# An attention-and-experts kernel: half block emptied by ACT, G two chunks later, the slot's search later, and the second layer two chunks behind the first

## The chip, the core and the metric

The kernel runs on one core of a Trainium2 chip. Of that core's engines the text uses these names: PE is the matrix engine (matmuls; its weight loads are shown apart as PEld), DVE the vector engine, ACT the scalar engine, POOL the general engine, SP the engine that issues most loads. Each engine works through its own list of instructions in the order in which they stand there. The metric is the device time of one execution in microseconds (us); lower is better.

## The reference

Two stages follow each other. The first is a Nystrom attention over 8 batches, 8 heads, 576 tokens and 64 numbers a head:

```python
A = sm(q, k_lm); Bm = sm(q_lm, k_lm); C = sm(q_lm, k)      # 32 landmarks
Z = Bm.transpose(0, 1, 3, 2) / (norm_1 * norm_inf + 1e-06)
for _ in range(6):
    Z = 2 * Z - Z @ Bm @ Z
attn_out = A @ Z @ C @ v
```

The second sends each token (512 numbers, all heads side by side) through one of 8 experts. A token takes the expert with the largest logit when it is the first of its batch or when its local gate is below 0.5, and otherwise keeps the expert of the token before it:

```python
h = np.maximum(x[b, s] @ w1[e], 0.0)        # 512 -> 1024
out[b, s] = p[e] * (h @ w2[e])              # 1024 -> 512
```

## The kernel before

**Batches and chunks.** The expert stage takes one batch after the other (`for b in range(B)`, B = 8). A batch is computed with one expert, the one that most of its tokens chose (`own`). Tokens that chose another are gathered over all batches into a "slot" of 128 rows that runs after batch 7 as a ninth, smaller expert (`sts[B]`). Further slots would follow in a loop at the end.

A batch's 576 tokens are done in two passes (`PASSES`): first 320 tokens, which are the output blocks 2 and 3 of 128 tokens and block 4 of only 64, the **half block**; then 256 tokens, blocks 0 and 1. Each pass has 8 **chunks** f, one for every 128 of the 1024 hidden numbers, so a batch has 16 chunks (`CH`). The text numbers them 0 to 15 within a batch, and b*16 + i over all. The slot has 8 chunks of 128 tokens.

**One chunk.** `mm1` (L525 on) is the first layer: six matmuls (L534) of weights `gh`, `gl` and tokens `ath`, `atl` into a bank of `ph`, of which there are two. High and low parts of a number are separate, so three products stand for one. ACT (L541) takes the positive part into `h`, DVE (L544, L547) its low part. `after` (L561 on) is the second layer: with the weights `wh`, `wl` of that chunk it adds three products for each full block to that block's `py` bank (L570), and for the half block two products to the one `pg` bank (L579), where 64 rows hold the high and 64 the low part. In `expert`, `before` holds the second layer of the preceding chunk: the program states the first layer of chunk f, then the second layer of chunk f-1. At the end of a batch `before()` finishes the last one.

**G.** Attention's last product is never formed by itself: `w_w1` (L487) multiplies the expert's `w1` by a small matrix of the batch into G, in two halves of 512 hidden numbers. Each half takes 16 matmuls (L498) into one `pg` bank and one `ph` bank, and two casts on ACT and two subtractions on DVE (L511, L512) empty them. As the `pg` bank is also the half block's, the first of these matmuls carries a dependency on the last reader of `pg`, kept in `reader["pg"]`. `G_AT` names the chunks of a batch at which the next batch's halves are stated.

**The store.** After the last chunk of a pass, `store` scales each block by the token's gate and writes it out. Full blocks are scaled by ACT (L593). For the half block DVE copies the 64 low rows out of `pg` (L596) and adds the 64 high ones (L597), then ACT scales (L599) and its queue issues the transfer. `ys` has two buffers.

**Weights.** `load_w2` loads a chunk's second-layer weights on SP's queue; ACT casts them to `wh` (L521) and POOL subtracts to get `wl` (L522). `get_w2` is called some chunks ahead.

**Attention beside it.** Attention of batch b+1 is cut into some 35 steps, put at chunk times in `events` by `at_time` and run just before the chunk whose time has passed (`run`). So are the slot's steps: `others` (L603) ranks the leftover tokens of all batches in a long row of DVE instructions, and `slot_tokens` (L669) searches the tokens of one slot in five pieces: the slot's batch and expert (`xregs`); a mask, then five `row` tiles of DVE (L695) with 8 matmuls each (L698) into one bank; addresses from it and 8 gathers on POOL (L721); two transposes on PE (L727); casts. `slot_weights` (L734) reads `xregs` on SP and loads that expert's `w1`.

**The order.** `schedule_with_timeline_sim=True`: what the program states is a priority, not the order. When the kernel is built, the order of every engine's list is settled with modelled durations: what the model holds ready goes first, the earlier stated first among these. `not_ahead_of` ties an instruction behind a marked one of its engine.

Of the kernel before, what the change touches and what calls it, by code (L numbers as in the profile page):

```python
# [9 lines left out]
F32 = mybir.dt.float32  # L10
F32R = mybir.dt.float32r
# [46 lines left out]
def nystrom_attn_then_sticky_moe(ctx, tc, qT, kT, v, wg, w12, out):  # L58
# [414 lines left out]
        nc.vector.tensor_mul(st["pw"], s[:, 0], s[:, 1])  # L473


    reader = {}

    def expert_of(reg):
        return nc.values_load(reg, engines=[ET.SP], min_val=0, max_val=E - 1,
# [45 lines left out]
    def mm1(st, f, s0, n, apart):  # L525

        hp = ph.tile([P, 512], F32, name="ph")[:, 0:n]
        gh, gl = st["g", f // 4]
        ah, al = st["at"]
        c = slice(f % 4 * P, f % 4 * P + P)  # L530
        i = 0
        for g in range(2):
            for w, x in ((gh, ah), (gh, al), (gl, ah)):
                nc.tensor.matmul(hp, w[:, g, c], x[:, g, s0:s0 + n], start=(i == 0), stop=(i == 5))  # L534
                i += 1

        m = n // P * P
        h = fk.tile([P, 640], F32R, name="h", bufs=3)
        x = fk.tile([P, P], F32R, name="hx", bufs=NC2) if apart and m < n else h[:, 2 * P:3 * P]
        e = m if apart else n  # L540
        nc.scalar.activation(out=h[:, 0:e], in_=hp[:, 0:e], func=AF.Relu)  # L541
        if e < n:
            nc.scalar.activation(out=x[:, 0:64], in_=hp[:, m:n], func=AF.Relu)
        nc.vector.scalar_tensor_tensor(out=h[:, 384:384 + m], in0=hp[:, 0:m], scalar=0.0, in1=h[:, 0:m].bitcast(F32),  # L544
                                       op0=ALU.max, op1=ALU.subtract)
        if m < n:
            nc.vector.scalar_tensor_tensor(out=x[:, 64:128], in0=hp[:, m:n], scalar=0.0, in1=x[:, 0:64].bitcast(F32),  # L547
                                           op0=ALU.max, op1=ALU.subtract)
        return h, x

    def expert(st, w2, passes, store, apart=False):

        before = None
        for s0, n, blocks in passes:
            yps, hs = {}, {}
            for f in range(NC2):
                hs[f] = mm1(st, f, s0, n, apart)
                if before:
                    before()

                def after(f=f, blocks=blocks, yps=yps, hs=hs):  # L561
                    full = [k for k in blocks if k < 4]
                    for k in full:
                        if k not in yps:
                            yps[k] = py.tile([P, DM], F32, name="py")
                    wh, wl = w2[f]
                    h = hs[f][0]
                    for part, w in ((0, wh), (0, wl), (384, wh)):
                        for i, k in enumerate(full):
                            nc.tensor.matmul(yps[k], h[:, part + i * P:part + i * P + P], w, start=(f == 0 and part == 0 and w is wh),  # L570
                                             stop=(f == NC2 - 1 and part == 384))
                    if 4 in blocks:


                        for ff in range(0 if f == NC2 - 1 else NC2, NC2) if apart else (f,):
                            if 4 not in yps:
                                yps[4] = pg.tile([P, DM], F32, name="pg")
                            for w in w2[ff]:
                                nc.tensor.matmul(yps[4], hs[ff][1], w, start=(ff == 0 and w is w2[ff][0]),  # L579
                                                 stop=(ff == NC2 - 1 and w is w2[ff][1]))  # L580
                    if f == NC2 - 1:
                        for k in blocks:
                            store(k, yps[k])

                before = after
                yield
        before()

    def store(b, st, k, yp):
        ys = fk.tile([P, DM], F32, name="ys", bufs=2)  # L590
        t0 = b * S + k * P
        if k < 4:
            nc.scalar.mul(out=ys, in_=yp, mul=st["pw"][:, k:k + 1])  # L593
            nc.scalar.dma_start(out=out[t0:t0 + P, :], in_=ys)
        else:
            nc.vector.tensor_copy(out=ys[0:64], in_=yp[64:128])  # L596
            last = nc.vector.tensor_tensor(out=ys[0:64], in0=ys[0:64], in1=yp[0:64], op=ALU.add)  # L597
            reader["pg"] = last.ins.name
            nc.scalar.mul(out=ys[0:64], in_=ys[0:64], mul=st["pw"][0:64, k:k + 1])  # L599
            nc.scalar.dma_start(out=out[t0:t0 + 64, :], in_=ys[0:64])  # L600


# [63 lines left out]
        xs.update(slot=slot, lo=lo, base=base, end=end, now=now, tabp=tabp)  # L666
        yield

    def slot_tokens(st):  # L669

        now = xs["now"]
        nc.vector.tensor_scalar_add(now, now, 1.0)
# [20 lines left out]
        for c0 in range(0, NCOL, 8):  # L693
            row = xp.tile([P, 8, P], BF16, name="row")
            nc.vector.tensor_tensor(out=row, in0=iota128.unsqueeze(1).broadcast_to([P, 8, P]),  # L695
                                    in1=xs["lo"][:, c0:c0 + 8].unsqueeze(2).broadcast_to([P, 8, P]), op=ALU.is_equal)
            for c in range(8):
                nc.tensor.matmul(pi, row[:, c, :], rhs[:, c0 + c, :], start=(c0 + c == 0), stop=(c0 + c == NCOL - 1))  # L698
        yield
        pf = xp.tile([P, 7], F32, name="pf")  # L700
        nc.vector.tensor_copy(out=pf, in_=pi)
# [22 lines left out]
        yield  # L724
        px = one.tile([P, 2, P])
        for g in range(2):
            nc.tensor.transpose(out=px[:, g, :], in_=xa[:, g].rearrange("p c l -> p (c l)"), identity=ident)  # L727
        st["at"] = [xp.tile([P, 2, P], F32R, name=f"xa{p}") for p in "hl"]
        nc.scalar.copy(out=st["at"][0], in_=px)
        nc.vector.tensor_tensor(out=st["at"][1], in0=px, in1=st["at"][0].bitcast(F32), op=ALU.subtract)  # L730
# [19 lines left out]
    def whole_slot():  # L750
# [9 lines left out]
        for f in range(NC2):  # L760
            w2[f] = load_w2(st["e"], f)
            next(gen)
        for _ in gen:
            pass


    sts = [{} for _ in range(B + 1)]
# [29 lines left out]

    CH, SPAN, END = 2 * NC2, 24, 4

    G_AT = (NC2 + 3, NC2 + 6)  # L800
    events = []

    def at_time(t, fn):
# [11 lines left out]
    def slots_begin():  # L815
        nonlocal xp
        lctx.close()
        xp = ctx.enter_context(tc.tile_pool(name="xp", bufs=1, side="right"))
        gens.extend([others(), slot_tokens(sts[B])])

    def slots_end():
        for _ in gens[1]:
            pass
        sts[B]["e"] = slot_weights(sts[B])

    xp, gens = None, []
    at_time((B - 2) * CH + END + 1, slots_begin)
    for i in range(4):
        at_time((B - 2) * CH + END + 2 + i, lambda: next(gens[0], None))
        at_time((B - 2) * CH + END + 6 + i, lambda: next(gens[1], None))  # L830
    at_time((B - 1) * CH + END + 0.5, slots_end)
    events.sort()

    def run(t):
# [17 lines left out]
    for b in range(B):  # L852
        st = sts[b]
        gen = expert(st, w2s[b], PASSES, lambda k, yp, b=b, st=st: store(b, st, k, yp), b == 0)
        for i in range(CH):
            if i < 2:
                get_w2(b, NC2 - 2 + i)
            elif i >= NC2 + 2:
                get_w2(b + 1, i - NC2 - 2)
            run(b * CH + i)  # L860
            if b == 0 and i == 2:

                w_w1(st, 1)
            if i in G_AT:
                w_w1(sts[b + 1], G_AT.index(i))
            next(gen)
        for _ in gen:
            pass
    run(B * CH)


    st = sts[B]
    gen = expert(st, w2s[B], ((0, P, (0,)),), lambda k, yp: slot_store(st, k, yp))
    for f in range(NC2):
        if f < 2:
            get_w2(B, NC2 - 2 + f)
        next(gen)
    for _ in gen:
        pass
    n_slots = nc.values_load(nslot[0:1, 0:1], min_val=0, max_val=E * B * 5)  # L880
    with tc.If(n_slots > 1):
        with tc.For_i(1, n_slots):
# [31 lines left out]
```

## Time and profile before

| what | us |
|---|---|
| median of three runs | 537.75 |
| lowest and highest | 537.05 and 537.84 |
| the profiled execution | 535.65 |
| its span, first to last instruction | 533.9 |
| PE busy in the span | 486.3 |
| DVE, ACT, POOL busy | 309.3, 209.6, 188.9 |

The profile is of one execution, taken by the chip's own recorder. Rows of a timeline give the start (us from the span's start), the duration, engine, line and operation, what it writes and reads, and in brackets the engine's idle time just before with what ended it. Rows of the waits give a sum in us, how often, and the longest. Rows of grouped lines give count, busy us, mean ns of one, idle us before. Windows give the busy us of each engine in a stretch, then the granted PE clock (1.00 is full speed) and transfers. Matmuls overlap, and their ends are modelled: the distance between starts is what one costs PE.

### The profile page before, as it was taken

The page shows a single profiled execution, that of the slowest core. Times are in us where ns is not written, and L with a number is a line of the kernel's source. Part 1 is how long each engine was busy: PE and PEld are TensorE (multiplying, and loading weights), DVE is VectorE, ACT ScalarE, POOL GpSimd, SP SyncE. Part 2 cuts the span into 40 slices and gives each one's busy share as a digit, 9 for nine tenths or more (in the row PEclk, how much of TensorE's full clock was granted, in tenths as well). Part 3 has the DMA queues.
Part 4 walks back from the last instruction along what each step waited for, and adds up shares of the span by engine and source line. Part 5 has one row for each costly group of instructions (what it writes and reads, how often), then busy time and mean ns, then how long its engine had stood idle before and what let it go on. Part 6 is the DMA issues. An engine that isn't in the chain of part 4 may idle for free. (4 is left out here: it accounts for less than half of the span.)

```text
span 533.9 us, 12288 instructions
## 1 busy us (share of the span) xinstructions
PE 486.3 (91%) x4791; PEld 349.9 (66%) x4791; DVE 309.3 (58%) x955; ACT 209.6 (39%) x529; POOL 188.9 (35%) x203
## 2 busy tenths in 40 slices
PE   6657569999999999999999999999998998799994
PEld 1325236866687577767786668657775787487784
DVE  7887837843587366834695368436653358752321
ACT  2333262444334451535245433354154412441451
POOL 5565270543126320643046301322133300563240
PEclk9775569999999999999999999999999999799999
DMA  8844760971159412961089010931083106371310
GB/s 300 328 147 172 247 211 6 372 262 40 51 183 355 139 51 69 376 231 51 3 325 329 24 50 28 353 119 51 1 284 109 68 1 223 128 267 44 109 60 19
DMA packets 38605, 82.59 MB, mean 155 GB/s; under 512 B 3163, under 2 KB 4443, under 8 KB 37776
## 3 DMA queue, kind: packets, MB, share of 16 engines
q1 hardware_dynamic: 30656, 66.22, 35.7%
q10 hardware_dynamic: 6400, 10.49, 5.4%
q0 software_dynamic: 1488, 5.07, 2.4%
q8 instruction: 39, 0.64, 0.5%
q14 instruction: 22, 0.18, 0.1%
HBM read 66.34 MB, written 15.47 MB: 153 GB/s over the span
## 5 line engine op out<-in xcount | busy, mean ns | idle before, releaser
L570 PE MATMUL py<-wh,h 128*128 128x512 f32 x528 | 177.4, 409 | 3.6 <-ACT h L541 2.9
L522 POOL TENSOR_TENSOR wl<-raw,wh 128x512 fp32r<-128x512 f32 x72 | 93.3, 1301 | 175.9 <-ACT wh L521 169.5
L541 ACT ACTIVATE h<-ph 128x256 fp32r<-128x256 f32 (+2 forms) x136 | 54.7, 403 | 146.7 <-PE ph L534 144.1
L570 PEld LDWEIGHTS py<-wh,h 128*128 128x128 f32 x528 | 91.4, 188 | 31.6 <-ACT h L541 12.8
L544 DVE SCALAR_TENSOR_TENSOR h<-ph,h 128x256 fp32r<-128x256 f32 (+1 forms) x136 | 55.3, 409 | 69.2 <-ACT h L541 68.0
L570 PE MATMUL py<-wl,h 128*128 128x512 f32 x264 | 88.1, 396 | 0.0
L534 PE MATMUL ph<-ath,gh 128*128 128x320 f32 (+1 forms) x256 | 79.1, 309 | 2.1 <-ACT gh L511 2.1
L534 PE MATMUL ph<-atl,gh 128*128 128x320 f32 (+1 forms) x256 | 76.6, 299 | 0.0
L534 PE MATMUL ph<-ath,gl 128*128 128x320 f32 (+1 forms) x256 | 76.1, 297 | 0.0
L521 ACT CAST wh<-raw 128x512 fp32r<-128x512 f32 x72 | 44.7, 620 | 54.4 <-PE py L570 40.3
L534 PEld LDWEIGHTS ph<-ath,gh 128*128 128x128 f32 x256 | 48.8, 191 | 19.7 <-issue 6.7
L570 PEld LDWEIGHTS py<-wl,h 128*128 128x128 f32 x264 | 49.5, 188 | 10.7 <-issue 1.3
L362 POOL TENSOR_TENSOR sa<-sa,mxa 128x1152 f32<-128x1152 f32 x8 | 17.1, 2132 | 107.8 <-DVE pall L473 102.7
L534 PEld LDWEIGHTS ph<-atl,gh 128*128 128x128 f32 x256 | 48.8, 191 | 6.6 <-issue 2.3
L534 PEld LDWEIGHTS ph<-ath,gl 128*128 128x128 f32 x256 | 48.7, 190 | 0.5 <-issue 0.3
L512 DVE TENSOR_TENSOR gl<-ph,gh 128x512 fp32r<-128x512 f32 x18 | 12.4, 688 | 36.0 <-ACT gh L511 36.0
L215 PE MATMUL one<-k_t,ql 64*32 64x288 f32 (+1 forms) x240 | 29.6, 483 | 1.6 <-ACT ql L192 1.0
L187 POOL TENSOR_TENSOR t<-k_t 128x288 f32<-128x288 f32 x28 | 20.1, 737 | 23.8 <-DVE sq L188 23.6
L498 PE MATMUL ph<-raw,wt 64*32 64x512 f32 x128 | 21.2, 658 | 4.9 <-DMA raw<-w 3.6
L219 DVE TENSOR_REDUCE mx<-one 128x1 f32<-128x288 f32 x30 | 13.5, 452 | 18.8 <-PE one L215 18.4
L187 POOL TENSOR_TENSOR t<-q_t 128x288 f32<-128x288 f32 x28 | 20.5, 752 | 9.8 <-DMA q_t<-qT 7.0
L579 PE MATMUL pg<-wh,h 128*128 128x512 f32 x56 | 23.1, 413 | 0.0
(283 smaller groups left out, 750.4 us busy)
## 6 DMA issues: line engine op xcount, KB each, us to landing
raw<-w SPq DMA_DIRECT2D x18, 1024.0 KB, 6.7
raw<-w SPq DMA_DIRECT2D x72, 256.0 KB, 5.8
v_t<-v SPq DMA_DIRECT2D x8, 1024.0 KB, 6.2
out<-ys ACTq DMA_DIRECT2D x32, 256.0 KB, 3.7
q_t<-qT SPq DMA_DIRECT2D x6, 1152.0 KB, 5.1
k_t<-kT SPq DMA_DIRECT2D x6, 1152.0 KB, 7.7
ad<-sa POOLq DMA_DIRECT2D x8, 576.0 KB, 6.2
q_t<-qT SPq DMA_DIRECT2D x4, 576.0 KB, 8.2
```

Of the source, the lines that this page charges most:

```text
L187: nc.gpsimd.tensor_add(t9[:, i], src[:, a + i, :, 0:9], src[:, a + i, :, 9:18])
L215: nc.tensor.matmul(pc[hf][32 * c:32 * c + 32, 0:n], st["ql"][r, h // 2, :], st["k"][r, h // 2, 288 * hf:288 * hf + n], start=True, stop=True)
L219: nc.vector.reduce_max(out=mx[:, hf:hf + 1], in_=pc[hf][:, 0:288], axis=AX.X)
L362: nc.gpsimd.tensor_tensor(out=sa, in0=sa, in1=mx.unsqueeze(2).broadcast_to([P, 2 * NJ, M]), op=ALU.subtract)
L498: mm = nc.tensor.matmul(ps[g][32 * c:32 * c + 32, :], st["wt"][r, g, 32 * c:32 * c + 32], w1[r, :, a * P:a * P + P], start=True, stop=True)
L521: nc.scalar.copy(out=wh, in_=raw)
L522: nc.gpsimd.tensor_tensor(out=wl, in0=raw, in1=wh.bitcast(F32), op=ALU.subtract)
L534: nc.tensor.matmul(hp, w[:, g, c], x[:, g, s0:s0 + n], start=(i == 0), stop=(i == 5))
L541: nc.scalar.activation(out=h[:, 0:e], in_=hp[:, 0:e], func=AF.Relu)
L544: nc.vector.scalar_tensor_tensor(out=h[:, 384:384 + m], in0=hp[:, 0:m], scalar=0.0, in1=h[:, 0:m].bitcast(F32), op0=ALU.max, op1=ALU.subtract)
L570: nc.tensor.matmul(yps[k], h[:, part + i * P:part + i * P + P], w, start=(f == 0 and part == 0 and w is wh), stop=(f == NC2 - 1 and part = ...
L579: nc.tensor.matmul(yps[4], hs[ff][1], w, start=(ff == 0 and w is w2[ff][0]), stop=(ff == NC2 - 1 and w is w2[ff][1]))
```

## The change

Four things are changed.

1. In `store`, ACT reads the half block's `pg` bank, twice, scaling on the way into `ys` and a new tile `yl`; POOL adds the two. `reader["pg"]` is now ACT's second instruction.
2. `G_AT` moves from chunks 11 and 14 to chunks 13 and 15.
3. The pieces of `slot_tokens` move from chunk times 106 to 109 (batch 6) to 112.5, 114.5, 115.5, 121.5 and 121.6 (batch 7), and `slot_weights` from 116.5 to 115. The search's matmuls are tied behind the first layer of chunk 113 and the transposes behind that of chunk 119.
4. The second layer follows two chunks behind the first. The list `behind` is shared by all batches, so a batch's last two second layers are stated after the next batch's first layers; `catch_up` empties it after the slot. `h` gets a fourth buffer, and `get_w2` calls come one chunk later, at the start of batch 0 too.

```diff
-    reader = {}
+    reader, behind = {}, []
...
-                nc.tensor.matmul(hp, w[:, g, c], x[:, g, s0:s0 + n], start=(i == 0), stop=(i == 5))
+                mm = nc.tensor.matmul(hp, w[:, g, c], x[:, g, s0:s0 + n], start=(i == 0), stop=(i == 5))
                 i += 1
+        marks["mm1", marks.setdefault("chunks", 0)] = mm.ins.name
+        marks["chunks"] += 1
...
-        h = fk.tile([P, 640], F32R, name="h", bufs=3)
+        h = fk.tile([P, 640], F32R, name="h", bufs=4)
...
-                if before:
-                    before()
+                if len(behind) == 2:
+                    behind.pop(0)()
...
-                before = after
+                behind.append(after)
                 yield
-        before()
+
+    def catch_up():
+        while behind:
+            behind.pop(0)()
...
-            nc.vector.tensor_copy(out=ys[0:64], in_=yp[64:128])
-            last = nc.vector.tensor_tensor(out=ys[0:64], in0=ys[0:64], in1=yp[0:64], op=ALU.add)
+
+            yl = fk.tile([P, DM], F32, name="yl", bufs=1)
+            p = st["pw"][0:64, k:k + 1]
+            nc.scalar.mul(out=ys[0:64], in_=yp[64:128], mul=p)
+            last = nc.scalar.mul(out=yl[0:64], in_=yp[0:64], mul=p)
             reader["pg"] = last.ins.name
-            nc.scalar.mul(out=ys[0:64], in_=ys[0:64], mul=st["pw"][0:64, k:k + 1])
+            nc.gpsimd.tensor_tensor(out=ys[0:64], in0=ys[0:64], in1=yl[0:64], op=ALU.add)
             nc.scalar.dma_start(out=out[t0:t0 + 64, :], in_=ys[0:64])
...
-                nc.tensor.matmul(pi, row[:, c, :], rhs[:, c0 + c, :], start=(c0 + c == 0), stop=(c0 + c == NCOL - 1))
+                mm = nc.tensor.matmul(pi, row[:, c, :], rhs[:, c0 + c, :], start=(c0 + c == 0), stop=(c0 + c == NCOL - 1))
+                not_ahead_of(mm, ("mm1", mark))
...
-            nc.tensor.transpose(out=px[:, g, :], in_=xa[:, g].rearrange("p c l -> p (c l)"), identity=ident)
+            tr = nc.tensor.transpose(out=px[:, g, :], in_=xa[:, g].rearrange("p c l -> p (c l)"), identity=ident)
+            not_ahead_of(tr, ("mm1", mark and mark + 6))
...
-    G_AT = (NC2 + 3, NC2 + 6)
+    G_AT = (NC2 + 5, NC2 + 7)
...
-        gens.extend([others(), slot_tokens(sts[B])])
+        gens.extend([others(), slot_tokens(sts[B], (B - 1) * CH + 1)])
...
-        at_time((B - 2) * CH + END + 6 + i, lambda: next(gens[1], None))
-    at_time((B - 1) * CH + END + 0.5, slots_end)
+
+    for t in (0.5, 2.5, 3.5, 9.5, 9.6):
+        at_time((B - 1) * CH + t, lambda: next(gens[1], None))
+    at_time((B - 1) * CH + 3, slots_end)
...
-            if i < 2:
-                get_w2(b, NC2 - 2 + i)
-            elif i >= NC2 + 2:
-                get_w2(b + 1, i - NC2 - 2)
+            if i < 3:
+                if b or i:
+                    get_w2(b, NC2 - 3 + i)
+            elif i >= NC2 + 3:
+                get_w2(b + 1, i - NC2 - 3)
```

More of the change, by code (lines that the diff above doesn't have):

```diff
@@ L551, in expert @@
     def expert(st, w2, passes, store, apart=False):
-        before = None
         for s0, n, blocks in passes:
@@ L667, in others, with slot_tokens @@
         yield
-    def slot_tokens(st):
+    def slot_tokens(st, mark=None):
         now = xs["now"]
@@ L762, in whole_slot @@
             next(gen)
-        for _ in gen:
-            pass
+        catch_up()
     sts = [{} for _ in range(B + 1)]
@@ L818, in slots_begin @@
         xp = ctx.enter_context(tc.tile_pool(name="xp", bufs=1, side="right"))
-        gens.extend([others(), slot_tokens(sts[B])])
+        gens.extend([others(), slot_tokens(sts[B], (B - 1) * CH + 1)])
     def slots_end():
-        for _ in gens[1]:
-            pass
         sts[B]["e"] = slot_weights(sts[B])
@@ L866, in nystrom_attn_then_sticky_moe @@
             next(gen)
-        for _ in gen:
-            pass
     run(B * CH)
@@ L874, in nystrom_attn_then_sticky_moe @@
     for f in range(NC2):
-        if f < 2:
-            get_w2(B, NC2 - 2 + f)
+        if f < 3:
+            get_w2(B, NC2 - 3 + f)
         next(gen)
-    for _ in gen:
-        pass
+    catch_up()
     n_slots = nc.values_load(nslot[0:1, 0:1], min_val=0, max_val=E * B * 5)
```

## The prediction

> **What bounds the kernel now.** I read the page first: its span, the engines' shares, and PE's busy tenths.
>
> ```profile
> span 533.9 us, 12288 instructions
> PE 486.3 (91%) x4791; PEld 349.9 (66%) x4791; DVE 309.3 (58%) x955; ACT 209.6 (39%) x529; POOL 188.9 (35%) x203
> ...
> PE   6657569999999999999999999999998998799994
> ```
>
> A slice is 13.3 us. From the seventh on PE is nearly always busy, so from about 80 us the time is what PE has to do plus its gaps; no other engine is above 58%. The change takes no matmul away, so it can only earn what lies in gaps. The chain of waits that ended last holds only the last 8 us and says nothing of them. I turned to PE's waits by cause (total us, times, longest).
>
> ```profile
> PE one L352 <- ACT ec L228: 5.1, 3, 2.7
> PE one L698 <- DVE rhs L691: 4.8, 1, 4.8
> ...
> PE py L570 <- ACT h L541: 2.9, 6, 0.9
> ...
> PE ph L498 <- DVE ys L597: 1.3, 2, 1.0
> ...
> PE one L727 <- DMA xa<-ad,gi: 1.0, 1, 1.0
> ```
>
> The last four all lie behind 80 us. The largest is the slot's search; the windows of that stretch (span, then busy us with counts for PE, PEld, DVE, ACT, POOL, then clock, transfers) show a second price.
>
> ```profile
> 440.00:450.00 10.00, 10.00 (x57) 8.65 (x56) 7.19 (x23) 3.90 (x7) 0.00 (x0) 1.00 0.47 154
> 450.00:460.00 10.00, 4.86 (x35) 2.52 (x35) 8.92 (x28) 3.00 (x5) 4.88 (x3) 0.70 0.75 271
> 460.00:470.00 10.00, 10.00 (x86) 7.58 (x84) 7.50 (x10) 5.06 (x11) 2.69 (x3) 0.96 0.34 92
> ```
>
> PE loses half of the middle window, and its granted clock falls to 0.70.
>
> **The search (part 3).** PE's timeline there, with a G half (16 matmuls L498) and a chunk elsewhere for comparison:
>
> ```profile
> 451.42 0.61 PE L570 MATMUL py<-wh,h 128*128 128x512 f32 x2
> 456.82 0.35 PE L698 MATMUL one<-rhs,row 128*128 128x7 bf16 x8 [4.78 <-DVE rhs L691]
> 457.53 1.06 PE L498 MATMUL ph<-raw,wt 64*32 64x512 f32 x1 [0.36 <-DVE ys L597]
> ...
> 459.42 0.58 PE L534 MATMUL ph<-ath,gh 128*128 128x256 f32 x1
> ...
> 460.87 0.36 PE L698 MATMUL one<-rhs,row 128*128 128x7 bf16 x8
> ```
>
> ```profile
> 115.01 0.61 PE L498 MATMUL ph<-raw,wt 64*32 64x512 f32 x1
> ...
> 116.03 0.38 PE L534 MATMUL ph<-ath,gh 128*128 128x256 f32 x1
> ...
> 512.63 0.28 PE L534 MATMUL ph<-ath,gh 128*128 128x256 f32 x1
> ...
> 513.34 0.63 PE L570 MATMUL py<-wh,h 128*128 128x512 f32 x2
> ...
> 514.73 0.22 PE L534 MATMUL ph<-xah,gh 128*128 128x128 f32 x1
> ```
>
> PE stands still for 4.78 us. After it the G half takes 457.53 to 459.42, 1.89 us, against 115.01 to 116.03, 1.02; the first layer takes 459.42 to 460.87, 1.45, against 512.63 to 513.34, 0.71. The slow clock thus cost 0.87 + 0.74 = 1.6. What PE waited for is a DVE row:
>
> ```profile
> 446.95 0.82 DVE L613 TENSOR_TENSOR_SCAN inc<-segs,one 128x320 f32<-128x320 f32 x1 [1.35 <-PE one L610]
> ...
> 453.08 1.21 DVE L695 TENSOR_TENSOR row<-iota,lo 128x1024 bf16<-128x1024 bf16 x1
> ...
> 456.33 0.43 DVE L691 TENSOR_TENSOR rhs<-tabp,mask 128x280 bf16<-128x280 bf16 x1
> ```
>
> From 446.95 to 456.76 DVE hardly rests: the ranking runs straight into the search, and PE's list had the search ahead of work that was ready. In the new order the search stands behind chunk 113, in batch 7, while the ranking stays in batch 6. At 2.1 us and more a chunk that is more than 10 us of cover, as much as the row is long. So 4.8 + 1.6 = **6.4** goes. What is late next is the search's own short row (mask, `rhs`, five `row` tiles of 1.21, one buffer), nothing of which waits for the ranking any more.
>
> The moved pieces also move POOL's gathers, SP's loads and the transposes:
>
> ```profile
> L721 POOL DMA_INDIRECT xa<-ad,gi x8 | 8.1, 1013 | 3.0 <-issue 1.8 <-DVE tis L713 0.8 <-PE ph L534 0.3
> ```
>
> ```profile
> xa<-ad,gi POOLq DMA_INDIRECT x8, 2.6
> ```
>
> The gathers take 8.1 + 3.0 = 11.1 on POOL and 2.6 to land, 13.7. They now start near chunk 116, and the transposes are stated at 121.5: a second-pass chunk is 0.71 + (514.73 - 513.34 = 1.39) = 2.1, and one of the first pass, by its wider first layer and its eight matmuls for six, 0.71 x 320/256 + 1.39 x 8/6 = 2.7; four of these and one and a half of those make 14.0. That is just enough: of the **1.0** for L727 I take all, 0 being the other end. On POOL nothing but the half block's add is due behind the gathers before chunk 123. On SP `slot_weights` waits for `xregs`, stated two chunks earlier; behind it are only weights due from chunk 123, so a late `xregs` costs nothing there.
>
> **The half block's bank and G (parts 1, 2).**
>
> ```profile
> L521 ACT CAST wh<-raw 128x512 fp32r<-128x512 f32 x72 | 44.7, 620 | 54.4 <-PE py L570 40.3 <-DMA raw<-w 12.6 <-PE pg L498 1.0
> ...
> L593 ACT ACTIVATE ys<-py,pall 128x512 f32<-128x512 f32 x32 | 20.3, 682 | 7.1 <-PE py L570 7.1
> ...
> L599 ACT ACTIVATE ys<-ys,pall 64x512 f32<-64x512 f32 x8 | 5.8, 724 | 6.1 <-DVE ys L597 6.0
> L596 DVE COPY ys<-pg 64x512 f32<-64x512 f32 x8 | 5.5, 693 | 5.4 <-DMA out<-ys 5.3
> L597 DVE TENSOR_TENSOR ys<-ys,pg 64x512 f32<-64x512 f32 x8 | 5.4, 679 | 0.3
> ```
>
> ```profile
> 403.38 0.69 DVE L596 COPY ys<-pg 64x512 f32<-64x512 f32 x1 [2.52 <-DMA out<-ys]
> ```
>
> Off DVE: 8 x (0.69 + 0.68) = 11.0. Onto ACT: eight more scalings of 0.72, 5.8. Onto POOL: eight adds of half height, whose nearest row is L522 of full height, 1.30; bounds 0.65 (half) and 1.30, and I take 1.30 since the elements per row are the same. All three are hidden at 58%, 39% and 35% busy. The wait for a free `ys` buffer (5.3 over four batches) moves from DVE to ACT. With G stated at chunk 13, four to five chunks behind the last reader of `pg`, PE's **1.3** at L498 goes. G at 13 is still three chunks, 6 us, ahead of its first use; its casts and subtractions (4 x 0.6 to 0.7) fit.
>
> **Two chunks behind (part 4).** Today a chunk's `h` has one second layer and one first layer of cover, 1.39 + 0.71 = 2.1 in the second pass; then twice that. The longest of the six waits for `h` was 0.9, when ACT first did G's casts. All **2.9** go; lower end 1.5, as the next row (`py` drained by two L593, 1.36) may still bind at the start of a pass. The fourth `h` buffer covers the longer life. At the end nothing changes: the last two second layers follow the last first layer today too.
>
> At the start, the loads for chunks 6 and 7 come a chunk later:
>
> ```profile
> 74.89 1.31 DVE L223 TENSOR_SCALAR nm<-mx 128x2 f32<-128x2 f32 x1
> ...
> 77.79 0.62 ACT L521 CAST wh<-raw 128x512 fp32r<-128x512 f32 x1 [1.91 <-DMA raw<-w]
> ...
> 79.22 1.17 PE L352 MATMUL one<-q_t,k_t 64*32 64x288 f32 x16 [2.07 <-ACT ec L228]
> ```
>
> DVE's `nm` was there at 76.2, but ACT stood before the cast of the last weights until 77.79, and PE got its bank back late. With the cast stated later, ACT may do the exponentials first. Ends: 0 (the order stays) and 1.9 (ACT's whole wait); I take **1.0**.
>
> **Against it.** Every list is ordered anew by modelled durations, so new small stalls will replace old ones. Ends: 0, and 5.2, what the old order has of such stalls (1.3 + 2.9 + 1.0); I take half, **2.6**.
>
> The Trainium skill (SBUF — State Buffer, "Who interferes with whom") speaks against the add on POOL: a DVE instruction with two SBUF inputs and a POOL instruction that reads SBUF exclude each other for a whole instruction. The trace agrees: the `row` beside POOL's subtraction took 1.79 where others took 1.21:
>
> ```profile
> 466.60 1.28 POOL L522 TENSOR_TENSOR wl<-raw,wh 128x512 fp32r<-128x512 f32 x1 [0.79 <-ACT wh L521]
> ...
> 467.18 1.79 DVE L695 TENSOR_TENSOR row<-iota,lo 128x1024 bf16<-128x1024 bf16 x1 [1.84 <-PE one L698]
> ```
>
> By that rule each add may hold DVE up for its length.
>
> **Sum.** 6.4 + 1.3 + 2.9 + 1.0 + 1.0 - 2.6 = 10.0 less. The profiled execution took 535.65 (span 533.9 and 1.75 around it), so 525.65 of its kind; it lies 2.1 below the median of 537.75, from which I forecast **527.7**. Its own range: best 12.6 + 0.9 = 13.5, so 524.2; worst 12.6 - 1.0 - 1.0 - 1.4 - 5.2 = 4.0, so 533.7.
>
> **The rivals.**
>
> *The search still holds PE.* The five `row` tiles share a buffer, so PE and DVE alternate; if the order puts nothing between, PE waits 5 x 1.21 = 6.1. For it: PEld waited for `row` today. Against it: PE itself did so only once, and batch 7 leaves DVE half idle. 10.0 - 6.1 = 3.9 less, 533.8.
>
> *The lag does not take effect*, because order follows modelled readiness. Then 2.9 and 1.0 (start) stay: 6.1 less, 531.6.
>
> *POOL's add holds DVE.* If each of eight adds makes DVE, and then PE, late by 1.30, that is 10.4, and 10.0 is gone: 538.1. Against it: DVE gets 11.0 us back. The Trainium skill's rule quoted above is what this rival would rest on.
>
> *ACT becomes the wall: slower.* At the end of a first pass ACT's list holds two scalings (1.36), the wait for `ys` (up to 2.52, on average 5.3 / 8 = 0.7), two half scalings (1.44) and a transfer that waits for POOL (1.30 or more). If no `h` is let in between, that is 4.1 without the `ys` wait. PE can go on until it needs a `ph` bank back: 1.39 + 0.71 + 1.39 = 3.5, less 0.4 on ACT and 0.4 on DVE, 2.7. The excess of 1.4 + 0.7 = 2.1, eight times, is 16.8 against 12.6 gained: 4.2 slower, 541.9. It decides from 12.6 / 8 = 1.6 excess a batch. For it: the transfer stands in ACT's own list. Against it: the order does let other work in, and ACT is 39% busy.
>
> **Chances.** Forecast 0.50, lag without effect 0.15, search still holding 0.15, POOL 0.05, ACT 0.15. A measurement tells about 0.2%, 1.1 us, from no change. Faster 0.80, within 0.05, slower 0.15. The range 523.0 to 535.0 holds the first three, leaving out the last two.
>
> **What would show it.** Right: no wait of PE for `rhs` or L597, clock 1.00 from 450 to 470, waits for `h` under 1, L352 near 79 gone, span near 524. Wrong: PE waits behind ACT's scalings at chunks 9 to 11, clock below 1 in batch 7, or a long wait at L727.

## The result: 519.9 us, and where the time went

| | us | runs |
|---|---|---|
| before, beside it on the same chip | 537.80 (537.05 to 540.33) | 4 |
| after | 519.94 (519.10 to 520.95) | 4 |
| forecast | 527.7 (523.0 to 535.0) | |

The ratio is 0.9661, with a 95% interval of 0.9625 to 0.9697. The kernel got faster by 17.9 us where 10.0 were forecast, and the time lies below the range.

The page of the changed kernel (span, PE's share, PE's tenths):

```profile
span 517.4 us, 12338 instructions
...
PE 475.5 (92%) x4791; PEld 346.2 (67%) x4791; DVE 300.0 (58%) x939; ACT 210.9 (41%) x537; POOL 198.0 (38%) x211
...
PE   6765668999999999999999999999999999699994
```

The number of matmuls is the same, 4791, but PE's busy time fell from 486.3 to 475.5. So 10.8 of the 16.5 us by which the span fell (533.9 to 517.4) came out of time in which PE counted as *busy*, where the prediction had looked for no more than the 1.6 of the slow clock. PE's waits (total us, times, longest) say what became of the gaps:

```profile
PE one L352 <- ACT ec L228: 4.1, 2, 2.1
...
PE ph L498 <- ACT yl L605: 3.4, 1, 3.4
...
PE ph L534 <- DVE gl L512: 1.7, 1, 1.7
PE one L736 <- DMA xa<-ad,gi: 1.5, 1, 1.5
```

The waits for `rhs`, for `h` and for L597 are gone. The transposes' wait (L727 before, L736 now) grew from 1.0 to 1.5, and two waits in batch 6 are new: G for ACT's emptying of the half block's bank, and the first layer for G's low part. Behind 80 us PE's waits add up to 10.03 in before and to 6.65 in after, so the gaps there gave 3.4.

Cutting each trace at the first matmul of each batch's first layer gives the time by batch:

| us | before | after | less |
|---|---|---|---|
| before batch 0 | 70.86 | 71.28 | -0.4 |
| batch 0 | 61.16 | 58.76 | 2.4 |
| batches 1 to 4, each | 57.57 to 57.82 | 54.54 to 54.70 | 12.2 in all |
| batch 5 | 56.87 | 53.75 | 3.1 |
| batch 6 | 52.13 | 51.48 | 0.7 |
| batch 7 | 43.17 | 44.62 | -1.5 |
| slot and end | 19.17 | 19.19 | 0.0 |

Windows of exactly one batch (span; busy us with counts for PE, PEld, DVE, ACT, POOL; clock, transfers): batches 2, 6 and 7 of before,

```profile
189.59:247.18 57.59, 57.23 (x569) 41.20 (x568) 34.83 (x112) 24.18 (x62) 20.78 (x19) 1.00 0.48 169
419.43:471.56 52.13, 46.99 (x329) 37.09 (x327) 34.52 (x106) 18.13 (x36) 11.45 (x8) 0.93 0.37 125
471.56:514.73 43.17, 41.60 (x244) 34.14 (x243) 13.09 (x39) 17.03 (x35) 18.21 (x16) 1.00 0.33 110
```

and the same batches of after:

```profile
184.58:239.12 54.54, 54.54 (x569) 40.34 (x567) 34.41 (x109) 24.49 (x64) 22.14 (x20) 1.00 0.50 178
402.11:453.59 51.48, 46.36 (x289) 36.57 (x286) 26.34 (x94) 17.89 (x37) 11.54 (x10) 0.93 0.39 131
453.59:498.21 44.62, 43.09 (x283) 34.66 (x282) 16.32 (x44) 16.78 (x35) 18.65 (x17) 1.00 0.30 95
```

Two things are to be seen. Batch 2 has the same 569 matmuls at the same full clock and is 3.05 shorter, although PE was idle there for only 57.59 - 57.23 = 0.36. And batch 6, from which the search was taken away (329 matmuls to 289), is hardly shorter: PE still stands idle for 51.48 - 46.36 = 5.1 of it, and the clock is still 0.93. So there are two questions: what "busy" time went away in the other batches, which are nearly all alike, and what holds batch 6.

**The busy time.** PE's groups by line (count, busy us, mean ns) name the groups that fell most; before:

```profile
L570 PE MATMUL py<-wh,h 128*128 128x512 f32 x528 | 177.4, 409 | 3.6 <-ACT h L541 2.9
...
L215 PE MATMUL one<-k_t,ql 64*32 64x288 f32 (+1 forms) x240 | 29.6, 483 | 1.6 <-ACT ql L192 1.0 <-ACT k_t L194 0.5
...
L251 PE MATMUL one<-v_t,ect 128*32 128x64 f32 (+1 forms) x640 | 19.2, 239 | 0.0
```

after:

```profile
L572 PE MATMUL py<-wh,h 128*128 128x512 f32 x528 | 167.7, 402 | 0.0
...
L215 PE MATMUL one<-k_t,ql 64*32 64x288 f32 (+1 forms) x240 | 22.7, 477 | 1.0 <-ACT k_t L194 0.8 <-ACT ql L192 0.2
...
L251 PE MATMUL one<-v_t,ect 128*32 128x64 f32 (+1 forms) x640 | 16.3, 238 | 0.0
```

Counts and the mean of one are almost the same; the sums are not, since matmuls overlap and a group's busy time is the time that it covers. PE's timeline shows why. Here the 80 matmuls of C times v (L251) stand in the second layer of batch 2, before,

```profile
223.79 0.30 PE L251 MATMUL one<-v_t,ect 128*32 128x64 f32 x2
224.02 0.50 PE L570 MATMUL py<-wh,h 128*128 128x512 f32 x1
224.35 0.39 PE L570 MATMUL py<-wl,h 128*128 128x512 f32 x1
224.59 0.40 PE L570 MATMUL py<-wh,h 128*128 128x512 f32 x1
224.91 0.30 PE L251 MATMUL one<-v_t,ect 128*32 128x64 f32 x2
...
226.04 1.72 PE L251 MATMUL one<-v_t,ect 128*32 128x64 f32 x76
227.68 0.73 PE L570 MATMUL py<-wh,h 128*128 128x512 f32 x2
```

and after:

```profile
217.87 1.73 PE L251 MATMUL one<-v_t,ect 128*32 128x64 f32 x80
219.53 0.73 PE L572 MATMUL py<-wh,h 128*128 128x512 f32 x2
```

Whole, the 80 take 219.53 - 217.87 = 1.66 from start to start. In three pieces they take 0.23 + 0.23 + 1.64 = 2.10: a piece of two matmuls costs 0.23, where two inside the long run cost 2 x 1.64/76 = 0.04. The three wide matmuls between two pieces take 224.91 - 224.02 = 0.89, where three cost 3 x 1.39/6 = 0.70 in an unbroken second layer: about 0.1 at each end. PE counts as busy all the while. The weight loads (PEld) of the same place in before show what is lost:

```profile
224.02 0.19 PEld L570 LDWEIGHTS py<-wh,h 128*128 128x128 f32 x1
224.13 0.19 PEld L570 LDWEIGHTS py<-wl,h 128*128 128x128 f32 x1
...
224.91 0.14 PEld L251 LDWEIGHTS one<-v_t,ect 128*32 128x32 f32 x2 [0.37 <-issue]
```

Inside the wide stretch a load starts 0.22 ahead of its matmul (224.13 for 224.35), beside the one in flight. The first load behind a change of shape starts together with its matmul (224.02, and 224.91 on the way back). Over batch 2 of before the median lead is 0.002 at the first matmul of a wide stretch and 0.22 inside. The Trainium skill (TensorEngine Tiling (Array Packing), "Key Properties") says that a change of the tiling mode drains the engine. The rows agree, at a price of about 0.1 a change here; no run took the load apart from the matmul.

All of batch 2, in before, in after and in a kernel with parts 1 and 2 alone (e4 below). A matmul's time here is the distance from its start to the next start on PE, waits included. From the wide stretches 38.70 is taken off, which is what their matmuls cost inside a stretch (0.146 for 320 columns, 0.119 for 256, 0.232 for 512):

| us | before | parts 1, 2 | after |
|---|---|---|---|
| wide stretches, beyond 38.70 | 3.57 | 4.01 | 2.49 |
| C times v (L251) | 2.10 | 2.11 | 1.66 |
| landmark scores and G (L215, L498) | 5.35 | 4.35 | 4.33 |
| inverse (L313, L320) | 2.90 | 2.39 | 2.40 |
| the other groups | 4.97 | 4.79 | 4.96 |
| sum | 18.89 | 17.65 | 15.84 |
| number of wide stretches | 20 | 24 | 15 |

So two things have a price. A wide stretch costs 0.17 to 0.18 beyond its matmuls in all three kernels, and after has five fewer of them: 1.1 of the 3.05. The other 2.0 lie in the small groups, which after leaves whole. The largest part is the landmark scores: in before two pieces of two scores each stood alone among wide matmuls and took 0.60 a piece, where all 16 take 1.16 in one run.

### The profile page after: what moved, and what is told of

Its sections match the earlier page's. It is cut to its first block, busy times and chain, and to the rows that moved or that the text cites. A ratio compares the mean times of both kernels' runs of the same rounds, so it can differ in the third digit from the quotient of the medians.

```text
span 517.4 us, 12338 instructions
## 1 busy us (share of the span) xinstructions
PE 475.5 (92%) x4791; PEld 346.2 (67%) x4791; DVE 300.0 (58%) x939; ACT 210.9 (41%) x537; POOL 198.0 (38%) x211
## 5 line engine op out<-in xcount | busy, mean ns | idle before, releaser
L572 PE MATMUL py<-wh,h 128*128 128x512 f32 x528 | 167.7, 402 | 0.0
L522 POOL TENSOR_TENSOR wl<-raw,wh 128x512 fp32r<-128x512 f32 x72 | 92.0, 1286 | 136.0 <-ACT wh L521 131.9
L572 PEld LDWEIGHTS py<-wh,h 128*128 128x128 f32 x528 | 93.0, 189 | 24.6 <-issue 9.5
L534 PE MATMUL ph<-ath,gh 128*128 128x320 f32 (+1 forms) x256 | 82.0, 320 | 3.9 <-ACT gh L511 2.2
L521 ACT CAST wh<-raw 128x512 fp32r<-128x512 f32 x72 | 44.6, 621 | 26.3 <-DMA raw<-w 11.5
L316 DVE TENSOR_TENSOR et<-et,one 128x64 f32<-128x64 f32 x42 | 9.0, 214 | 37.3 <-ACT et L315 37.2
L498 PE MATMUL ph<-raw,wt 64*32 64x512 f32 x128 | 19.6, 644 | 6.8 <-DMA raw<-w 3.4
L215 PE MATMUL one<-k_t,ql 64*32 64x288 f32 (+1 forms) x240 | 22.7, 477 | 1.0 <-ACT k_t L194 0.8
L352 PE MATMUL one<-q_t,k_t 64*32 64x288 f32 x248 | 19.1, 471 | 4.1 <-ACT ec L228 4.1
```

Source lines behind the costliest of these rows:

```text
L215: nc.tensor.matmul(pc[hf][32 * c:32 * c + 32, 0:n], st["ql"][r, h // 2, :], st["k"][r, h // 2, 288 * hf:288 * hf + n], start=True, stop=True)
L352: nc.tensor.matmul(pa[g][32 * c:32 * c + 32, 0:288], st["k"][r, h // 2, S:S + M], st["q"][r, h // 2, 288 * hf:288 * hf + 288], start=True, ...
L498: mm = nc.tensor.matmul(ps[g][32 * c:32 * c + 32, :], st["wt"][r, g, 32 * c:32 * c + 32], w1[r, :, a * P:a * P + P], start=True, stop=True)
L521: nc.scalar.copy(out=wh, in_=raw)
L522: nc.gpsimd.tensor_tensor(out=wl, in0=raw, in1=wh.bitcast(F32), op=ALU.subtract)
L534: mm = nc.tensor.matmul(hp, w[:, g, c], x[:, g, s0:s0 + n], start=(i == 0), stop=(i == 5))
```

## The experiments

Each "before" ran beside its experiment on the same chip, with medians of 537.2 to 537.9. Batch lengths are from each kernel's profile.

**First round: which part brought it, and is it the number of breaks?** The first theory was that the time goes with the number of wide stretches and that only the lag of two chunks makes these fewer. The rival was that the broken small groups cost as much themselves, so that G's new place can bring it too.

e1, the whole change with the second layer one chunk behind (four `h` buffers and the later weights stay):

```diff
-                if len(behind) == 2:
+                if len(behind) == 1:
```

> The changed kernel with the second layer one chunk behind again, all else kept. Theory S (fewer stretches): the two-chunk lag lets PE do small attention matmuls in whole groups; in the changed kernel PE goes from wide to small matmuls 15 times a batch, in this one 20 to 21 times as in the kernel before, and batches 1 to 4 are 57 us long again instead of 54.5. Six batches by 2.5 to 3 us: 534 to 538 us. Theory F (as forecast): the lag only takes away waits for h of 2.9 us and 1.0 at the start: 523 to 525 us.

Measured: 521.33, ratio 0.9672 (0.9629 to 0.9716). The count of stretches went back up, to 21, and batch 1 took 55.15, yet nearly all of the gain stayed. The time lies below both expectations, so the theory that the lag is what brings it fell.

e2, before with part 4 alone; e3, before with part 3 alone; e4, before with parts 1 and 2 alone (their lines of the diff above, nothing else):

> The kernel before with the two-chunk lag alone (four h buffers, weights a chunk later), search, G and the half block's bank as before. Theory S: 15 to 16 stretches a batch, nearly the whole gain: 520 to 523 us, batches 1 to 4 at 54.5 to 55.5 us. Theory F: 533 to 535 us.

> The kernel before with the slot's search moved alone. Theory S with U (the stall of batch 6 has a second cause right under the first: ACT stands before the cast of batch 7's weights until they land, and with it the emptying of the bank that G needs): PE still stands 3 us or more in batch 6, and batch 7 gets longer by 1 to 1.5: 536 to 539 us. Theory F: the stall and its slow clock go, 6.4 less: 531 to 532 us.

> The kernel before with the half block's bank emptied by ACT and G two chunks later alone. Its PE list has 24 stretches of small matmuls in batches 1 to 5 where the kernel before has 20. Theory S: 4 more a batch in five batches, at 0.2 to 0.56 us each, 4 to 11 us more, less the 1.3 of the wait for the bank: 540 to 548 us. Theory F: 1.3 less: 536 to 537 us.

| kernel | us | ratio | batch 1 | batch 6 | batch 7 |
|---|---|---|---|---|---|
| e2: lag, `h`, weights | 524.10 | 0.9740 (0.9705 to 0.9776) | 56.67, then 52.83 in turns | 52.87 | 42.42 |
| e3: search later | 537.74 | 0.9998 (0.9973 to 1.0022) | 57.59 | 52.27 | 44.20 |
| e4: bank and G | 525.73 | 0.9789 (0.9756 to 0.9821) | 56.35 | 50.74 | 41.71 |

e4 missed both of its expectations. It has *more* wide stretches than before, 24 for 20, and is 12 us faster: the count alone is not the price. By the table of batch 2, the wide stretches cost 0.4 more in e4, but G at chunks 13 and 15 and the landmark scores now stand whole (1.0 less), and so does the inverse (0.5 less). e2 came out 1.1 above what was expected of it, with batches of 54.7 in the mean. e2 and e4 earn 13.8 and 12.1 alone and 17.9 together with part 3, so the two largely save the same time.

e3 is the plain miss: the search, the largest term of the forecast, earns nothing by itself. Its trace has a longer wait in the same batch under another name. PE's largest wait in e3 (total, times, longest):

```profile
PE ph L498 <- DVE ys L599: 8.0, 3, 6.5
```

There PE waits to begin G, for the half block's bank, which in e3 DVE empties (L598, L599). DVE's timeline shows why that comes late:

```profile
454.49 1.21 DVE L697 TENSOR_TENSOR row<-iota,lo 128x1024 bf16<-128x1024 bf16 x1
...
456.36 1.32 DVE L691 TENSOR_SCALAR mask<-slot,now 128x40 bf16<-128x40 f32 x1
457.71 0.69 DVE L598 COPY ys<-pg 64x512 f32<-64x512 f32 x1
...
458.80 0.43 DVE L693 TENSOR_TENSOR rhs<-tabp,mask 128x280 bf16<-128x280 bf16 x1
459.26 0.68 DVE L599 TENSOR_TENSOR ys<-ys,pg 64x512 f32<-64x512 f32 x1
```

From 448.36 to 459.94 DVE has no idle time. The ranking stands first in its list, then come the search's first `row`, `mask` and `rhs`, which still ran in batch 6 since only the search's matmuls are tied, and the emptying stands among them. Before had the same under the search's wait: its G, at 457.53, waited for L597, which ended at 457.47, 0.7 behind `rhs`.

```profile
456.79 0.68 DVE L597 TENSOR_TENSOR ys<-ys,pg 64x512 f32<-64x512 f32 x1
```

What stood next in PE's list was not ready either, so taking away the first wait alone could earn next to nothing. That DVE's list is the cause in e3 is read from the trace; no run moved it by itself.

A third engine stood still in that stretch: ACT, before a cast of batch 7's second-layer weights that had not landed, for 5.92 in e3 and for 6.08 in before:

```profile
455.67 1.91 ACT L521 CAST wh<-raw 128x512 fp32r<-128x512 f32 x3 [5.92 <-DMA raw<-w]
```

```profile
454.43 1.92 ACT L521 CAST wh<-raw 128x512 fp32r<-128x512 f32 x3 [6.08 <-DMA raw<-w]
```

In neither of the two does PE's long wait name ACT. In after it does, because part 1 has given the emptying of the bank to ACT. ACT's and then PE's and SP's timeline of that place in after:

```profile
440.04 0.62 ACT L521 CAST wh<-raw 128x512 fp32r<-128x512 f32 x1 [4.07 <-DMA raw<-w]
440.68 0.69 ACT L604 ACTIVATE ys<-pg,pall 64x512 f32<-64x512 f32 x1
441.38 0.68 ACT L605 ACTIVATE yl<-pg,pall 64x512 f32<-64x512 f32 x1
```

```profile
442.12 0.61 PE L498 MATMUL ph<-raw,wt 64*32 64x512 f32 x1 [3.37 <-ACT yl L605]
```

```profile
429.33 1.03 SPq L484 DMA_DIRECT2D raw<-w  x2
430.61 16.87 SPq L519 DMA_DIRECT2D raw<-w  x8
```

The weights are issued at 430.61, right behind the two large loads of `w1`, and the first cast can begin at 440.04, 9.4 later. ACT empties the half block's bank only then, and G and with it PE wait for that bank. Windows of 10 us (span, busy, clock, transfers) show PE at 6.14 and the clock at 0.68 there, as low as in the stall of before:

```profile
440.00:450.00 10.00, 6.14 (x40) 3.86 (x48) 2.19 (x5) 5.80 (x11) 7.46 (x6) 0.68 0.56 178
```

So the second theory: batch 6 has several causes of nearly the same length, and the search was only one of them.

**Second round: the parts, and both theories tested by themselves.** e5, part 2 alone; e6, the whole change without part 3; e7, the whole change with batch 7's weights behind G:

```diff
-            if i < 3:
+            if b == B - 2 and i >= NC2 + 3:
+                for f in {14: (0, 1), 15: (2,)}.get(i, ()):
+                    get_w2(b + 1, f, ("gh", "relu"))
+            elif b == B - 1 and i < 5:
+                get_w2(b, NC2 - 5 + i)
+            elif i < 3:
```

There `get_w2` ties those casts on ACT behind G's casts and the newest positive part. The loads of these weights are stated two to three chunks later too, but SP issued them right behind those of `w1` all the same, from 432.36. e8 is the opposite of the gain: after, with C times v stated in five pieces of 16, a chunk apart:

```diff
+            if k == 18 and b > 1:
+                for p in range(5):
+                    at_time(start + SPAN * k / n + p, lambda b=b, p=p: c_v(sts[b], p))
+                continue
             at_time(start + SPAN * k / n, step)
```

> The kernel before with G two chunks later alone; the half block's bank is emptied by DVE as before. Theory P (pieces: PE's time beside its wide matmuls grows with every place where a group of small matmuls is broken up or mixed with another): G at its old chunks came among the landmark scores and broke both; later it does not, whoever empties the bank. 524 to 529 us, batches 1 to 4 near 56.4 us as with bank and G together. Rival B (the bank's emptying by ACT is what earned it): 536 us or more.

> The changed kernel with the slot's search at its old place, all else kept. Theory P: the search's move only puts its five breaks into batch 7 and the wait for the gathers stays; batch 7 gets 1 to 2 us shorter, batch 6 about as much longer or less: 517 to 521 us, no slower than the changed kernel. Theory F (as forecast, the move earns the 6.4 of stall and slow clock): 525 to 527 us.

> The changed kernel with, in batch 6 alone, the casts of batch 7's weights stated at chunks 14 and 15 and tied on ACT behind G's casts and the newest first layer's (the loads themselves are not held). Theory U (PE's stall in batch 6 is ACT standing before a cast whose weights have not landed): the waits of 3.4 and 1.7 us shrink to under 2 together and the slow clock goes: 513 to 516 us. Rival L (what PE waits for there is the load of the expert's first layer, or the choice of the expert): the stall stays within 1 us: 519 to 521 us.

> The changed kernel with one group of small matmuls (C times v, L251, batches 2 to 7) stated in five pieces a chunk apart, each tied behind the first layer of the chunk before; the matmuls are the same. PE goes to small matmuls 19 times a batch instead of 15, 18 in batch 0. Theory P: each further piece costs 0.3 to 0.45 us (0.2 at the wide matmuls around it, the rest in the group): 23 pieces, 7 to 10 us: 527 to 531 us. Rival N (breaks cost nothing, the batches are short for another reason): 519 to 521 us.

| kernel | us | ratio | batch 1 | batch 6 | batch 7 |
|---|---|---|---|---|---|
| e5: G alone | 525.21 | 0.9783 (0.9745 to 0.9821) | 56.35 | 51.11 | 41.71 |
| e6: without part 3 | 520.75 | 0.9694 (0.9676 to 0.9711) | 54.54 | 55.36 | 41.85 |
| e7: weights behind G | 514.18 | 0.9559 (0.9525 to 0.9593) | 54.54 | 45.25 | 45.15 |
| e8: C times v in pieces | 527.97 | 0.9826 (0.9807 to 0.9846) | 56.25 | 50.91 | 44.42 |

e5 is e4 without the bank's new way, and takes as long: that ACT empties the bank (part 1) earns nothing that can be seen in the time; moving G does it.

e7 takes ACT's stand away, both waits of PE with it, and batch 6 falls by 51.48 - 45.25 = 6.2. The window at the same place has PE at 8.85 and the clock at 1.00:

```profile
440.00:450.00 10.00, 8.85 (x71) 5.76 (x69) 6.17 (x16) 5.85 (x13) 7.16 (x6) 1.00 0.59 198
```

So the size of the stall was read about rightly in the prediction; what had to go for it to be earned was not the search alone.

e6 shows the other half. Its waits have two causes one after the other in batch 6, the search's `row` and the bank:

```profile
PE one L703 <- DVE row L700: 5.1, 1, 5.1
...
PE ph L498 <- ACT yl L602: 3.3, 1, 3.3
```

Batch 6 is 3.9 longer than in after, but batch 7, with no search in it, is 2.8 shorter. In the whole, part 3 is worth 0.8 (520.75 to 519.94, with overlapping intervals).

e8 measures the price of a piece. A batch grows by 56.25 - 54.54 = 1.71, with four more places where C times v breaks into wide work, for example:

```profile
223.00 0.30 PE L255 MATMUL one<-v_t,ect 128*32 128x64 f32 x2
223.23 0.50 PE L580 MATMUL py<-wh,h 128*128 128x512 f32 x1
...
224.12 0.42 PE L255 MATMUL one<-v_t,ect 128*32 128x64 f32 x14
```

Two matmuls (L255 there) again cost 0.23 and the three wide ones 0.89, as in before. Counted as in the table of batch 2, 0.79 of the 1.71 lie at the wide stretches, 0.2 for each of the four, and 0.48 in C times v: 0.3 a piece in all. The rest is not the pieces' own: in the new order one half of G was broken up by landmark scores and the inverse, and took 1.54 where whole it takes 1.02. The number of matmuls is unchanged, and in batches 1 to 5 PE waits for none of it.

**Third round: a search in one piece.** In e7 the search still breaks batch 7's wide work in several places. e9 is e7 with five `row` buffers, the 40 matmuls in one run behind chunk 114, and the transposes behind chunk 122. e10 is the whole change without part 4.

```diff
-            row = xp.tile([P, 8, P], BF16, name="row")
+            row = rows[c0] = xp.tile([P, 8, P], BF16, name="row", bufs=5)
...
+        for c0, row in rows.items():
             for c in range(8):
...
-                not_ahead_of(mm, ("mm1", mark))
+                not_ahead_of(mm, ("mm1", mark and mark + 1))
```

> The kernel with the weights behind G, and in it the slot's search whole: the five row tiles have a buffer each, their 40 matmuls are tied in one row behind chunk 114, and the transposes come two chunks later (tied behind chunk 122). Theory P: 6 breaks in batch 7 instead of 9, 0.3 to 0.45 us each, and the wait of 1.4 us for the gathers gone: 2.3 to 2.8 us less than that kernel's 514.2, so 511.4 to 511.9. Rival N: breaks cost nothing, 1.4 less: 512.8; if the matmuls now wait for the last row tile instead: 514 or more.

> The changed kernel with the whole of part 4 undone: one chunk behind, three h buffers, weights loaded as before. Its PE list has 24 stretches a batch, where the one-behind kernel with four buffers has 20 to 21. Theory P: batches 1 to 4 near 56.4 us as with G alone, search without gain: 524.5 to 527.5 us. Rival K (the one-behind kernel's 521.3 came from the search together with G, not from four buffers and later weights): 520 to 522.5 us.

e10 took 524.76, ratio 0.9770 (0.9728 to 0.9812), with batch 1 back at 56.35 and 24 stretches. e9 took 517.86, ratio 0.9644 (0.9612 to 0.9676). Batch 7 did what was expected, 45.15 to 42.52, but batch 6 lost far more, 45.25 to 52.15. The timelines of POOL, DVE, ACT and PE in e9 show a cause that was not in the expectation:

```profile
438.64 5.99 POOL L609 TENSOR_TENSOR ys<-ys,yl 64x512 f32<-64x512 f32 x1 [29.92 <-ACT yl L607]
```

```profile
437.65 2.34 DVE L706 TENSOR_TENSOR row<-iota,lo 128x1024 bf16<-128x1024 bf16 x2
...
440.03 3.48 DVE L706 TENSOR_TENSOR row<-iota,lo 128x1024 bf16<-128x1024 bf16 x3
```

```profile
445.18 0.59 ACT L511 CAST gh<-ph 128x512 fp32r<-128x512 f32 x1 [6.61 <-POOL ys L609]
```

```profile
446.59 1.22 PE L574 MATMUL py<-wh,h 128*128 128x512 f32 x2 [5.75 <-ACT h L545]
```

With five buffers nothing parts the `row` instructions any more, and DVE runs them one behind the other, in batch 6. The half block's add on POOL, 1.32 in e7, takes 5.99 beside them. ACT's transfer of `ys` stands in ACT's list and waits for the add, everything behind it waits too, and PE comes to rest for 5.75.

**Fourth round: the rows moved out of the add's way.** e11 is e9 with the `row` instructions tied on DVE behind the low part of chunk 113, so that they run in batch 7; e12 is e11 with the second layer one chunk behind.

```diff
+        marks["low", marks["chunks"] - 1] = low.ins.name
...
+            not_ahead_of(dv, ("low", mark))
```

> The kernel with the search whole, its five row tiles on DVE tied behind the first layer of chunk 113. Theory D (in that kernel the five rows, run one behind the other in batch 6, held POOL's add of the half block for 6.0 us instead of 1.3, ACT's transfer behind it for 6.6, and with it PE for 5.7): the add is back at 1.3, batch 6 at 45 to 46 us as with the weights behind G, batch 7 stays at 42.5: 511 to 513 us. Rival C (the stall came from the change of order elsewhere): batch 6 stays at 50 or more, 516 to 518 us.

> The same kernel with the second layer one chunk behind. Of all changes the lag itself is undecided: one behind was 521.3 (517.7 to 521.9) against 519.9. Theory P: 20 to 21 breaks a batch instead of 15, at 0.6 us a batch by the traces of those two, and 1.5 in batch 0: 2 to 5 us more than with two behind, 513 to 518 us. Rival Z (the lag is worth nothing beside the rest): within 1 us of it, 510 to 514 us.

e11 took 514.78, ratio 0.9568 (0.9544 to 0.9591). The add was back at its old length (eight of them, busy us and mean ns, and idle before):

```profile
L610 POOL TENSOR_TENSOR ys<-ys,yl 64x512 f32<-64x512 f32 x8 | 10.3, 1284 | 52.0 <-ACT yl L608 51.6
```

and batch 6 was down to 46.54. The total missed its expectation: batch 7 took 43.93, not 42.5, and batches 6 and 7 together are worth no more than in e7 (90.47 to 90.40). e7 and e11 are as fast as each other, and both beat the change. e12 took 515.90, ratio 0.9596 (0.9574 to 0.9619): the lag by itself is worth about 1.1 here, and 1.4 between e1 and after, both with overlapping intervals, so whether the total gains by it stays open. In the traces of both pairs two chunks behind is 0.6 shorter in batches 1 to 3 and 1.3 to 1.5 in batch 0, but longer in batch 5 (0.7 and 1.3) and in batch 7 (2.0 and 0.6).

The medians as a ladder: before 537.8; G later 525.2; with ACT emptying the bank 525.7; with the search later 524.8; with the fourth `h` buffer and the later weights 521.3; with the lag 519.9; with batch 7's weights behind G 514.2. A step of about 1 us or less is not told from none, and the steps hang on their order: part 4, the last two before e7, earned 13.8 by itself (e2).

## Why the prediction was wrong

The direction was right. The step that failed is the premise, "The change takes no matmul away, so it can only earn what lies in gaps." Batches 1 to 4 alone became 12.2 shorter, with the same matmuls. In batch 2 the idle time before was 0.36 of the 3.05 that went; the rest lay in time that the tenths show as 9. What a matmul costs PE depends on its neighbours, and the order changed in every batch. e8 leaves the work as it is, breaks groups up and gives 8.0 of the 17.9 back; e4 and e10, with 24 stretches each, show that the number of breaks is not all: how whole the small groups are counts for more, 2.0 of batch 2's 3.05. The prediction quoted starts of matmuls and used them as the same at every place; a comparison of one group's distance between starts in two places of the trace (0.23 for two matmuls, 0.04 within the run) would have shown it.

Term by term:

- **Search, 6.4.** Two steps failed. "PE's list had the search ahead of work that was ready": next in the list stood G, which was not ready until DVE's L597 had ended, 0.7 behind `rhs`, as the prediction's own line at 457.53 shows. And "In the new order the search stands behind chunk 113" held for its matmuls, not for its part on DVE. Alone the move earned 0 (e3), within the change about 0.8 (e6). The question asked was what is late next in the search; the one to ask was what is late next *for PE*, in the same stretch: DVE's emptying of the bank, and once ACT had that, ACT's stand before L521. The size was about right, and by luck: e7 earned 6.2 in batch 6, by taking away another stall than the one that was summed.
- **Bank, 1.3.** The wait for L597 went in batch 5 with G's move (e5 has none there), but in batch 6 there is a longer one for the same bank, 2.5 in e5 and 3.4 in after.
- **Waits for `h`, 2.9.** Right: none is left in after, and with the lag undone (e1) 3.6 are there.
- **Transposes, 1.0.** Wrong: 1.5 remain. The cover of 14.0 for 13.7 was too thin to count on; with the transposes behind chunk 122 the wait is gone (e9, e11).
- **Start, 1.0.** Wrong: the wait at L352 near 79 is 2.0 (2.07 before); ACT still casts ahead of the exponentials, which was the lower end named.
- **New stalls, 2.6.** The part in batch 6 belongs to the search's term. Outside it the new waits are small, the 0.5 at the transposes among them.

The two errors have opposite signs. The terms that were counted brought less than 10.0 (the gaps behind 80 us gave 3.4), and the uncounted broken groups brought more than was missing. Of the rivals, none gave the time. The lag did take effect. The POOL add did not hold DVE: the low parts of `h` beside it took 0.42 to 0.43, as they did in before, and of the 11.0 that were to leave DVE its busy time lost 9.3. ACT as the wall and POOL's add, each dismissed for its own reason, came together in e9, by one chain: DVE held POOL, POOL held ACT's transfer, ACT held PE.

Of the signs named in advance, "no wait of PE for `rhs` or L597" and "waits for `h` under 1" came true; "L352 near 79 gone" and "clock 1.00" did not (0.68 in the window 440 to 450, the same place of the program); "span near 524" came out at 517.4.

## What to carry to other kernels

Before calling PE's busy time fixed, compare the distance between starts of one group of matmuls where it runs whole and where it is broken up among matmuls of another shape; if they differ, keeping such groups whole can be worth more than closing gaps, as it was here. When a wait is to be removed, look at what stands next in that engine's list and when it becomes ready, and at every other engine in the same stretch for a chain that ends nearly as late, above all one that works without a pause or stands before a transfer. And take a new engine in a chain (here POOL between ACT's scaling and ACT's transfer) as a wait in all the lists through which it passes.

## What the runs showed of the hardware

- A change between small-tile and full-array matmuls costs PE about 0.1 at each end of the wide stretch, and a piece of two small matmuls 0.23 instead of 0.04. An extra piece cost about 0.3 in all (e8), and no idle time shows it.
- A run of DVE instructions with two SBUF inputs can hold a POOL instruction for nearly all of its length: 5.99 for an add of 1.32, beside five `row` instructions. The Trainium skill (SBUF — State Buffer, "Who interferes with whom") says that such instructions exclude each other for a whole instruction, and that the order of issue decides who is blocked. The trace agrees, and goes further: the add began at 438.64 and ended at 444.63, while the last of the five ended at 443.51, so POOL got no turn between them, and the price was several instructions, not one. The add's own turn then held DVE: L663, beside its end, took 1.12 (443.57 to 444.69), where the same step took 0.18 in before.
- In batch 6 the granted clock, over 10 us, fell with PE's stall: 0.70 in before, 0.68 in after, 0.74 in e9, against 1.00 in e7, where the longest wait of PE left in batch 6 is 1.15. Here a stall that only changed its name kept this second price.
